# Attention, experts and feed-forward in one kernel: other places for operands, another order of weight splits, routing on GpSimd, stores by turns

## The chip, the cores and the metric

The kernel runs on one core of a Trainium2 chip. A core has TensorE (PE, with its weight load shown apart as PEld), VectorE (DVE), ScalarE (ACT), GpSimd (POOL) and SyncE (SP, which here only issues DMAs). The metric is the time on the device in microseconds (us), the median of the runs shown.

## What is computed

Three layers follow one another. Attention over 2 batches of 8 heads, 768 positions of 64 numbers, in which a query sees only the keys of its own cluster; a mixture of 8 experts in which each of 1536 tokens goes to one expert (512 to 1024 to 512); and a feed-forward layer (512 to 2048 to 512) whose activation is a quotient of two polynomials. All in fp32.

```python
mask = q_assign[:, :, :, None] == k_assign[:, :, None, :]     # argmax over 16 centroids
scores = np.where(mask, scale * np.matmul(q, k.transpose(0, 1, 3, 2)), -1000000000.0)
x = softmax(scores) @ v                                       # then (1536, 512)

expert_idx = np.argmax(xn @ en.T / tau, axis=1)
for e in range(E):
    mask = expert_idx == e
    out[mask] = gate_w[mask, None] * (np.maximum(x[mask] @ w1[e], 0.0) @ w2[e])

h = x @ w_in
P = a[0] + a[1] * h + a[2] * h**2 + a[3] * h**3
Q = 1.0 + np.abs(b[0]) * np.abs(h) + np.abs(b[1]) * h**2
return (P / (Q + 1e-06)) @ w_out
```

## The kernel before

**Split products.** A product in fp32 is made of three products of `fp32r` halves: an operand is split into a high part (a cast) and a low part (the operand less its high part), and PE multiplies high by high, high by low and low by high. Nearly all work of the other engines is such splitting. All instructions of one engine run in the order in which the program is written (`manual_schedule`), and each engine waits for the others by semaphores.

**Attention, 0 to about 287 us.** A unit is one head and one half of the queries (three blocks of 128); there are 32, and each takes six slots `t`, one for each block of 128 keys. In slot `t` PE transposes a block of probabilities (`transp`, L467); for the first block of a unit ScalarE copies it to `ptc` (L472, one buffer), GpSimd makes its high part `phi` and its low part `plo` (L72, L483); for the five others ScalarE casts `phi` (L475) and DVE subtracts (`plo`, L485). PE multiplies both with the values (L495, L496). At the end of a unit `pv_out` copies the sums of products and adds 1e-9 to the sum of exponentials (`ssum`: on GpSimd, L507, with a reciprocal on DVE six slots later, L512; on DVE, L504, with the reciprocal at once for the last two units, `FK`). `finish` divides, on DVE.

The task table `at(slot, fn)` puts everything else into the slots: heads' operands (`QBs`, `KBs`, `QAs`, `KAs`, three sets in turn, in the space of weight chunks 2 and 3 and three places beside them), the words of the feed-forward weights, routing, and the first expert's four weight chunks: `load_ahead` issues a chunk's load from SyncE into one of three `wraw` buffers, `early_hi` and `early_lo` split a quarter of it into the space of chunk 0 to 3 (L191 and L72 the casts, L197 the low parts). `early_split` does both.

**Routing** (`route`, a generator that is advanced now and then) takes three blocks of tokens at once: the largest logit, a one-hot row of it (L587, its fp32 copy L588), and its product with the token number (L590); then PE sums the one-hots, and GpSimd works out positions (L622, L623). The groups of batch 0 fall into the middle of attention, the last group of batch 1 behind its end.

**Experts, to about 476 us.** Expert 0 in part runs inside the end of attention (`eb_...`, L682). Experts 1 to 7 have four steps each: `expert_in`, `expert_relu` (high part on ScalarE, L1218, low part on DVE, L1220), `expert_out` of the step before. `weights(n)` splits the next `n` quarters of the ring of eight chunks (ScalarE L112, DVE L117), as far as their places are free. `row_gates` (the generators in `later`) works out the gate of an expert's rows: ScalarE reads the rows `xr` (L647), after which GpSimd may gather the next expert's rows into the same buffer (L666) and raises a sum to a power (L648).

**Feed-forward, to 752 us.** Three groups of four blocks of tokens, 16 steps each: `ff_in` (L1282), `poly_2` of the step before (ScalarE's logarithm and exponential L1430 and L1431, DVE L1432 to L1434), now and then a gather and transposes for the next group (`transpose_y`, L1265, with L1268 and L1270 on DVE), `poly_1` (ScalarE, DVE L1308 and L1310, GpSimd L1309), `poly_3` (splits the quotient: ScalarE L1442, GpSimd L1443 in the first group), `ff_out` three steps behind (L1455 to L1457), and `wide_part`, which splits quarters of the feed-forward weights from `yraw` (ScalarE L112, DVE L117). `ff_in` of a step takes one of two PSUM buffers, which L1310 of two steps before has read last. The loop's last line before is:

```python
            if i:
                wide_part(2 if i % 2 else 1)
```

At the end of a group the four results are copied and stored: by GpSimd's scatter in groups 0 and 1, from SyncE in the last group; the last block of all in two halves, one copied and stored by ScalarE, one copied by DVE and stored from SyncE.

## Time and profile before

| | |
|---|---|
| median of 3 runs | 761.67 us (760.78 to 762.51) |
| the profiled execution | 760.98 us, its span 759.3 us |
| PE busy | 734.6 us (97%) |
| DVE busy | 593.3 us (78%) |
| ACT busy | 565.0 us (74%) |
| POOL busy | 367.7 us (48%) |
| granted TensorE clock | 0.998 |

The span runs from the first to the last instruction of the profiled execution; 1.7 us of its time lie around it. A row of the timeline names start, length, engine, line, operation, what it writes and reads, and in brackets how long the engine had been idle and whose work ended that.

### The profile page before, as it was taken

How to read it: one execution, taken by the hardware profiler on the slowest of the kernel's cores; microseconds unless marked ns; L12 is line 12 of the kernel's file. 1: busy time of each engine (PE TensorE's matmuls, PEld its weight loads, DVE VectorE, ACT ScalarE, POOL GpSimd, SP SyncE). 2: the span in 40 equal slices, each digit the busy share in tenths (PEclk: the TensorE clock that was granted, in tenths of full speed). 3: DMA queues.
4: the chain of work that ended last, by engine and by line, in shares of the span. 5: the costliest groups of instructions: out<-in, count | busy, mean ns of one | idle time of the engine just before them, and what ended most of it. 6: DMA issues, size and time to landing. Idle time of an engine off the chain costs nothing.

```text
span 759.3 us, 12608 instructions
## 1 busy us (share of the span) xinstructions
PE 734.6 (97%) x4283; PEld 633.0 (83%) x4283; DVE 593.3 (78%) x1127; ACT 565.0 (74%) x1127; POOL 367.7 (48%) x462
## 2 busy tenths in 40 slices
PE   8999999999999999999999999999999999999996
PEld 5889999888889977889989999777888888888884
DVE  7778888898888877886676555589978788787774
ACT  5778888888888875885577555688877777777773
POOL 6798987888778872030221101266555332242220
PEclk9999999999999999999999999999999999999999
DMA  5677877867788265796775366222001110010001
GB/s 148 183 203 197 238 202 200 265 187 200 217 245 258 72 202 174 251 334 235 278 245 196 135 200 196 73 85 85 15 0 42 44 28 1 1 56 1 1 0 59
DMA packets 48712, 109.20 MB, mean 144 GB/s; under 512 B 6937, under 2 KB 10777, under 8 KB 48642
## 3 DMA queue, kind: packets, MB, share of 16 engines
q1 hardware_dynamic: 45618, 98.65, 42.4%
q0 software_dynamic: 2880, 9.55, 4.2%
q8 instruction: 35, 0.57, 0.3%
q14 instruction: 35, 0.29, 0.1%
q10 hardware_dynamic: 144, 0.13, 0.1%
HBM read 76.06 MB, written 18.99 MB: 125 GB/s over the span
## 4 chain that ended last, share of the span: by engine, by line
PE 71%; DVE 11%; ACT 6%; issue 4%; POOL 4%; DMA 3%; SPq 0%; POOLq 0%; ACTq 0%; DVEq 0%
PE pg L1282 14%; PE ph L1211 9%; PE pr L1457 5%; PE pr L1455 5%; PE pr L1456 5%; PE pt L467 4%; PE py L1242 3%; PE py L1241 3%; PE py L1240 3%; PE po_acc L495 2%; PE ps L449 2%; PE po_acc L496 2%; PE ps L450 2%; DVE plo L485 2%; DVE nm L452 2%
## 5 line engine op out<-in xcount | busy, mean ns | idle before, releaser
L1309 POOL TENSOR_TENSOR Bt<-Bt,A 128x512 f32<-128x512 f32 x46 | 59.7, 1297 | 147.4 <-ACT Bt L1307 147.4
L485 DVE TENSOR_TENSOR plo<-pt,phi 128x384 fp32r<-128x384 f32 x160 | 87.9, 550 | 20.9 <-ACT phi L475 18.4
L467 PE MATMUL pt<-ident,pr 128*128 128x128 f32 x576 | 96.3, 276 | 7.8 <-DVE plo L485 6.0
L475 ACT CAST phi<-pt 128x384 fp32r<-128x384 f32 x160 | 76.8, 482 | 32.2 <-PE pt L467 30.9
L1282 PE MATMUL pg<-x2hi,ck 128*128 128x512 f32 x368 | 92.7, 394 | 2.7 <-DVE Ct L1310 2.7
L452 DVE TENSOR_REDUCE nm<-ps 128x1 f32<-128x768 f32 x96 | 91.2, 950 | 5.3 <-PE ps L450 5.0
L458 ACT ACTIVATE pr<-ps,nm 128x768 f32<-128x768 f32 x96 | 87.4, 910 | 6.1 <-DVE nm L452 5.6
L467 PEld LDWEIGHTS pt<-ident,pr 128*128 128x128 f32 x576 | 70.7, 140 | 22.5 <-DVE plo L485 13.4
L1282 PEld LDWEIGHTS pg<-x2hi,ck 128*128 128x128 f32 x368 | 68.8, 188 | 19.4 <-DVE Ct L1310 4.0
L117 DVE TENSOR_TENSOR ck<-wraw,ck 128x512 fp32r<-128x512 f32 x112 | 71.1, 685 | 10.0 <-ACT ck L112 9.9
L1455 PE MATMUL pr<-ck,ghi 128*128 128x512 f32 x192 | 76.2, 397 | 0.0
L1457 PE MATMUL pr<-ck,glo 128*128 128x512 f32 x192 | 75.5, 393 | 0.0
L1456 PE MATMUL pr<-ck,ghi 128*128 128x512 f32 x192 | 75.4, 392 | 0.0
L495 PE MATMUL po_acc<-phi,vhl 128*128 128x384 f32 x192 | 72.9, 380 | 0.0
L496 PE MATMUL po_acc<-plo,vhl 128*128 128x384 f32 x192 | 65.0, 339 | 1.1 <-DVE plo L485 1.0
L112 ACT CAST ck<-wraw 128x512 fp32r<-128x512 f32 x112 | 62.5, 623 | 3.6 <-DMA wraw<-in_w_dram 3.3
L648 POOL TENSOR_TENSOR gss<-gss,half 128x2 f32<-128x2 f32 (+1 forms) x8 | 6.2, 777 | 119.8 <-ACT px L647 104.5
L1211 PE MATMUL ph<-xhi,ck 128*128 128x256 f32 x448 | 62.6, 282 | 0.0
L1432 DVE SCALAR_TENSOR_TENSOR Bt<-Bt,A 128x512 f32<-128x512 f32 (+1 forms) x48 | 32.7, 682 | 37.3 <-ACT A L1431 37.0
L1211 PEld LDWEIGHTS ph<-xhi,ck 128*128 128x128 f32 x448 | 59.0, 188 | 2.2
L1430 ACT ACTIVATE A<-Bt,qc 128x512 f32<-128x512 f32 (+1 forms) x48 | 34.3, 716 | 22.2 <-POOL Bt L1309 22.2
L1282 PE MATMUL pg<-x2lo,ck 128*128 128x512 f32 x184 | 49.9, 393 | 0.0
(331 smaller groups left out, 1937.6 us busy)
## 6 DMA issues: line engine op xcount, KB each, us to landing
wraw<-in_w_dram SPq DMA_DIRECT2D x32, 1024.0 KB, 6.4
words<-in_w_in_dram SPq DMA_DIRECT2D x16, 512.0 KB, 7.2
wf_d<-wz SPq DMA_DIRECT2D x32, 256.0 KB, 4.2
words<-in_w_out_dram SPq DMA_DIRECT2D x16, 512.0 KB, 7.4
yraw<-wf_d SPq DMA_DIRECT2D x16, 512.0 KB, 4.1
operands<-operands SPq DMA_DIRECT2D x40, 192.0 KB, 3.9
kq<-in_kqT_dram SPq DMA_DIRECT2D x16, 384.0 KB, 6.1
ys_d<-ysb SPq DMA_DIRECT2D x15, 260.0 KB, 4.3
```

What stands on the lines that cost most here:

```text
L452: dve.tensor_reduce(nm, ps[:, :, :HS], axis=AX.XY, op=ALU.max, negate=True)
L458: act.activation(pr.rearrange("p (a s) -> p a s", a=2), ps[:, :, :HS], AF.Exp, bias=nm[:, 0:1], accum_out=st["sum", u][:, qb:qb + 1])
L467: pe.transpose(t[:, j, :], st["P", u][j][:, kb * P:(kb + 1) * P], ident)
L475: act.copy(phi, tv)
L485: dve.tensor_tensor(plo, tv, phi.bitcast(F32), op=ALU.subtract)
L495: pe.matmul(o, w, phi, start=(kb == 1), stop=False)
L496: pe.matmul(o, w, plo, start=False, stop=(kb == 0))
L1211: pe.matmul(ph[:, f2, :], w[:, wx, k, c0:c0 + P], x[:, k, :], start=(i == 0), stop=(i == len(ops) - 1))
L1282: pe.matmul(ph, w[:, wx, k, c0:c0 + P], x[:, k, :], start=(i == 0), stop=(i == len(ops) - 1))
L1455: pe.matmul(o, ghi[:, s_], w[:, 0, k, :], start=(fb == 0), stop=False)
L1456: pe.matmul(o, ghi[:, s_], w[:, 1, k, :], start=False, stop=False)
L1457: pe.matmul(o, glo[:, s_], w[:, 0, k, :], start=False, stop=(fb == F2B - 1))
```

## The change

1. **Operands.** The three sets of a head's operands get other places in the space of chunks 2 and 3: set 0 now lies wholly in that of chunk 3, sets 1 and 2 in that of chunk 2, but for `QAs[2]`. The last head, 15, has set 0.
2. **End of attention.** Chunk 0 is split in slots 161 to 167 instead of 165 to 173; then chunk 2 in slots 171 to 177, ahead of chunk 1 in 175 to 180, with ScalarE and GpSimd taking the casts by turns and GpSimd all low parts; before, chunk 2 came last, and two of its low parts were on DVE. Chunk 3's casts stand in slots 183 to 187 instead of 191 to 193, and the three loads in slots 169, 184 and 187 instead of 174, 187 and 191.
3. **Sums.** For the last six units the 1e-9 is added on DVE, with the reciprocal at once; before, for the last two.
4. **Routing.** For batch 0's groups the one-hot, its copy and its product are made by GpSimd, in four operations instead of three on DVE. `dst_all` (L1270) goes from DVE to GpSimd too.
5. **First experts.** In the first four steps the ReLU stands ahead of the weights, in the first one `row_gates`' first part too; in expert 1 each `weights` call splits two quarters instead of three.
6. **Wide weights.** `wide_part` is not run in steps 1 and 2 and splits two quarters in steps 3 to 7, 9 and so on; before, two and one by turns from step 1.
7. **Last stores.** In the last group blocks go by turns from SyncE and ScalarE; the last block is copied whole by ScalarE and stored by it.

```diff
@@ -285,9 +285,9 @@
     scale = float(D) ** -0.5
     w2_, w3_ = (pools[j].tile([P, 8, 512], F32R, name=f"operands{j}", tag=f"ck{j}").rearrange("p a f -> p (a f)")
                 for j in (2, 3))
-    QBs = [w2_[:, j * S:(j + 1) * S] for j in range(3)]
-    KBs = [w2_[:, 3 * S:4 * S], w2_[:, 4 * S:5 * S], w3_[:, 0:S]]
-    QAs = [w3_[:, j * S:(j + 1) * S] for j in range(1, 4)]
+    QBs = [w3_[:, S:2 * S], w2_[:, 0:S], w2_[:, S:2 * S]]
+    KBs = [w3_[:, 2 * S:3 * S], w2_[:, 2 * S:3 * S], w2_[:, 3 * S:4 * S]]
+    QAs = [w3_[:, 3 * S:4 * S], w2_[:, 4 * S:5 * S], w3_[:, 0:S]]
     w0_ = pools[0].tile([P, 8, 512], F32, name="logits", tag="ck0")
     Ls = [w0_[:, j, 0:2 * NB * C].rearrange("p (g c) -> p g c", c=C) for j in range(2)]
     wz_ = [hp.tile([P, 512], I32, name=f"wz{j}", bufs=1) for j in range(6)]
@@ -500,7 +500,7 @@
         act.copy(ob, st["O", u])
         st["ob", u] = ob
         s = st["sum", u]
-        if u in FK:
+        if u >= n - 6:
             dve.tensor_scalar(s, s, 1e-9, None, op0=ALU.add)
             recip(u)
         else:
@@ -569,6 +569,7 @@
             return xpool.tile([P, 3, E], dt, name=name)
 
         last = k0 + 3 == NBT
+        eng = dve if b else pool
         rows = slice(g * 3, g * 3 + 3)
         dve.tensor_tensor(lt, lg2[:, rows, :, 0], lg2[:, rows, :, 1], op=ALU.add)
         store_x(b, g, slice((H - 1) * D, W))
@@ -584,10 +585,15 @@
         dve.tensor_reduce(m2, v, axis=AX.X, op=ALU.max)
         yield
         ohb = rE("rohb", BF16)
-        dve.tensor_tensor(ohb, v, m2.to_broadcast([P, 3, E]), op=ALU.is_equal)
-        dve.tensor_copy(oh, ohb)
+        if eng is dve:
+            dve.tensor_tensor(ohb, v, m2.to_broadcast([P, 3, E]), op=ALU.is_equal)
+            dve.tensor_copy(oh, ohb)
+        else:
+            pool.tensor_tensor(v, v, m2.to_broadcast([P, 3, E]), op=ALU.subtract)
+            pool.tensor_scalar(oh, v, 1.0, 0.0, op0=ALU.add, op1=ALU.max)
+            p_copy(ohb, oh)
         ot = rE("rot")
-        dve.tensor_tensor(ot, oh, tok1[:, k0:k0 + 3].unsqueeze(2).to_broadcast([P, 3, E]), op=ALU.mult)
+        eng.tensor_tensor(ot, oh, tok1[:, k0:k0 + 3].unsqueeze(2).to_broadcast([P, 3, E]), op=ALU.mult)
         yield
         yield True
 
@@ -986,15 +992,14 @@
         for j in range(3):
             at(131 + 12 * j, load_ahead, j)
         for j in range(4):
-            at((165, 167, 170, 173)[j], early_split, 0, j, pool, pool)
-            at((175, 177, 179, 181)[j], early_split, 1, j, pool, pool)
-            at((183, 185, 186, 187)[j], early_hi, 2, j, act)
-            at((184, 186, 187, 188)[j], early_lo, 2, j, dve if j > 1 else pool)
-        at(174, load_ahead, 3)
-        at(187, load_ahead, 4)
-        at(191, load_ahead, 5)
+            at((161, 163, 165, 167)[j], early_split, 0, j, pool, pool)
+            at((171, 172, 174, 177)[j], early_split, 2, j, (act, pool, pool, act)[j], pool)
+            at((175, 176, 179, 180)[j], early_split, 1, j, (pool, pool, act, pool)[j], pool)
+        at(169, load_ahead, 3)
+        at(184, load_ahead, 4)
+        at(187, load_ahead, 5)
         for j in range(3):
-            at(191 + j, early_hi, 3, j, act)
+            at((183, 185, 187)[j], early_hi, 3, j, act)
         at(144, first_rows_2)
         at(147, eb_gather)
         at(163, eb_x)
@@ -1267,7 +1272,7 @@
         act.copy(hi[:, :, c], t)
         dve.tensor_tensor(lo[:, :, c], t, hi[:, :, c].bitcast(F32), op=ALU.subtract)
         if k < SB:
-            dve.tensor_tensor(dst_all[:, k:k + 1], y[:, DM:DM + 1], never_all[:, k:k + 1], op=ALU.add)
+            pool.tensor_scalar(dst_all[:, k:k + 1], y[:, DM:DM + 1], never_all[:, k:k + 1], 1.0, op0=ALU.add, op1=ALU.mult)
 
     def ff_in(gi, fb):
         hi, lo = x2[gi]
@@ -1369,20 +1374,22 @@
             if p == FB // 2 - 1 and e + 1 < E:
                 transpose_x(e + 1)
             passed.add(("in", e, p))
+            if i < 4:
+                expert_relu(e, p)
             if i == 0:
-                expert_relu(e, p)
-            weights(3)
+                next(later[0])
+            weights(2 if e == 1 else 3)
             if e == E - 1:
                 expert_relu(e, p)
                 if p > 1:
                     for tb in range(2):
                         transpose_y(0, 2 * (p - 2) + tb, x2b)
-            if 0 < i and e < E - 1:
+            if 3 < i and e < E - 1:
                 expert_relu(e, p)
             if i:
                 expert_out(*steps[i - 1])
                 passed.add(("out", *steps[i - 1]))
-            weights(3)
+            weights(2 if e == 1 else 3)
             if e > 5:
                 wide_part(3, 4)
             if p == FB // 2 - 1 and e + 1 < E:
@@ -1460,22 +1467,14 @@
                 if tb % 2 == 0:
                     op["o"] = yraw[0].tile([P, 2, DM], F32, name="yraw", bufs=3)
                 y = op["o"][:, tb % 2]
-                if b == NBT - 1:
-                    half_ = slice(DM // 2, DM)
-                    act.activation(y[:, half_], o[:, half_], AF.Copy, scale=-1.0)
-                    act.dma_start(outs[NBT][b * P:(b + 1) * P, half_], y[:, half_])
-                    half_ = slice(0, DM // 2)
-                    dve.tensor_scalar(y[:, half_], o[:, half_], -1.0, None, op0=ALU.mult)
-                    sp.dma_start(outs[NBT][b * P:(b + 1) * P, half_], y[:, half_])
-                    continue
-                if tb % 2:
+                if tb % 2 and b < NBT - 1:
                     dve.tensor_scalar(y, o, -1.0, None, op0=ALU.mult)
                 else:
                     act.activation(y, o, AF.Copy, scale=-1.0)
                 if b < SB:
                     scatter(y, dst_all[:, b:b + 1], b)
                 else:
-                    sp.dma_start(outs[NBT][b * P:(b + 1) * P, :], y)
+                    (act if tb % 2 else sp).dma_start(outs[NBT][b * P:(b + 1) * P, :], y)
 
     left = nc.values_load(cnt_i[0:1, NBT:NBT + 1], min_val=0, max_val=NT)
     qc = const.tile([P, 1], F32, name="qc")
@@ -1498,8 +1497,8 @@
                 poly_3(*steps[i - 1])
             if i >= LAG:
                 ff_out(*steps[i - LAG])
-            if i:
-                wide_part(2 if i % 2 else 1)
+            if 3 <= i < 8 or i % 2:
+                wide_part(0 if i == 1 else 2)
         poly_2(*steps[-1])
         ff_out(*steps[-3])
         poly_3(*steps[-1])
```

PE's instructions stand in the same order before and after. Where the others change is shown at three places.

GpSimd, end of attention, before: `ck_4289` is chunk 1, `ck_4434` chunk 2; each pair of `phi` and `plo` is the first block of a unit.

```order
L72 TENSOR_SCALAR ck_4289<-wraw 128x512
L197 TENSOR_TENSOR ck_4289<-wraw,ck_4289 128x512
L507 TENSOR_SCALAR ssum<-ssum 128x3
L72 TENSOR_SCALAR ck_4289<-wraw 128x512
L197 TENSOR_TENSOR ck_4289<-wraw,ck_4289 128x512
L72 TENSOR_SCALAR ck_4289<-wraw 128x512
L197 TENSOR_TENSOR ck_4289<-wraw,ck_4289 128x512
L72 TENSOR_SCALAR phi<-ptc 128x384
L483 TENSOR_TENSOR plo<-ptc,phi 128x384
L72 TENSOR_SCALAR ck_4289<-wraw 128x512
L197 TENSOR_TENSOR ck_4289<-wraw,ck_4289 128x512
L507 TENSOR_SCALAR ssum<-ssum 128x3
```

And after (`ck_4219` is chunk 2, `ck_4298` chunk 1):

```order
L197 TENSOR_TENSOR ck_4219<-wraw,ck_4219 128x512
L72 TENSOR_SCALAR ck_4219<-wraw 128x512
L197 TENSOR_TENSOR ck_4219<-wraw,ck_4219 128x512
L72 TENSOR_SCALAR phi<-ptc 128x384
L483 TENSOR_TENSOR plo<-ptc,phi 128x384
L72 TENSOR_SCALAR ck_4219<-wraw 128x512
L197 TENSOR_TENSOR ck_4219<-wraw,ck_4219 128x512
L72 TENSOR_SCALAR ck_4298<-wraw 128x512
L197 TENSOR_TENSOR ck_4298<-wraw,ck_4298 128x512
L72 TENSOR_SCALAR ck_4298<-wraw 128x512
L197 TENSOR_TENSOR ck_4298<-wraw,ck_4298 128x512
L197 TENSOR_TENSOR ck_4219<-wraw,ck_4219 128x512
```

The sums L507 are gone from between the pieces, and chunk 2's pieces stand ahead of chunk 1's.

ScalarE, first two steps of expert 1, before (`ck_...` are weight chunks, L647 reads the rows):

```order
L1218 ACTIVATE hhi<-ph 128x512
L112 CAST ck_4988<-wraw 128x512 x4
L112 CAST ck_4999<-wraw 128x512 x2
L647 ACTIVATE px_5005,gss_5006<-xr 128x512 x2
L112 CAST ck_4999<-wraw 128x512 x2
L112 CAST ck_5045<-wraw 128x512
L1218 ACTIVATE hhi<-ph 128x512
L112 CAST ck_5045<-wraw 128x512 x3
L112 CAST ck_5101<-wraw 128x512 x3
L1218 ACTIVATE hhi<-ph 128x512
```

And after (L647 is now L653, L1218 is L1223):

```order
L1223 ACTIVATE hhi<-ph 128x512
L653 ACTIVATE px_4991,gss_4992<-xr 128x512 x2
L112 CAST ck_5000<-wraw 128x512 x4
L1223 ACTIVATE hhi<-ph 128x512
L112 CAST ck_5042<-wraw 128x512 x4
L662 ACTIVATE gv_4994,gmx_4993<-gv_4994,gss_4992 128x8 x2
L1223 ACTIVATE hhi<-ph 128x512
L112 CAST ck_5098<-wraw 128x512 x4
```

The two readers of `xr` stand ahead of the casts that they followed, and each ReLU has four casts behind it.

DVE, start of the feed-forward loop, from L1308 of step 1 on, before:

```order
L1308 TENSOR_TENSOR Ct<-Ct,px_6910 128x512
L1310 SCALAR_TENSOR_TENSOR Ct<-Ct,ab,px_6910 128x512
L117 TENSOR_TENSOR ck_6950<-yraw,ck_6950 128x512 x2
L1432 SCALAR_TENSOR_TENSOR Bt<-Bt,A 128x512
L1433 SCALAR_TENSOR_TENSOR A<-Bt,A 128x512
L1434 SCALAR_TENSOR_TENSOR Ct<-Ct,ab,A 128x512
L1308 TENSOR_TENSOR Ct<-Ct,pg 128x512
L1310 SCALAR_TENSOR_TENSOR Ct<-Ct,ab,pg 128x512
L117 TENSOR_TENSOR ck_6950<-yraw,ck_6950 128x512
L1432 SCALAR_TENSOR_TENSOR Bt<-Bt,A 128x512
L1433 SCALAR_TENSOR_TENSOR A<-Bt,A 128x512
L1434 SCALAR_TENSOR_TENSOR Ct<-Ct,ab,A 128x512
```

And after (L1308, L1310 and L1432 to L1434 are now L1313, L1315 and L1439 to L1441):

```order
L1313 TENSOR_TENSOR Ct<-Ct,px_6912 128x512
L1315 SCALAR_TENSOR_TENSOR Ct<-Ct,ab,px_6912 128x512
L1439 SCALAR_TENSOR_TENSOR Bt<-Bt,A 128x512
L1440 SCALAR_TENSOR_TENSOR A<-Bt,A 128x512
L1441 SCALAR_TENSOR_TENSOR Ct<-Ct,ab,A 128x512
L1313 TENSOR_TENSOR Ct<-Ct,pg 128x512
L1315 SCALAR_TENSOR_TENSOR Ct<-Ct,ab,pg 128x512
L1439 SCALAR_TENSOR_TENSOR Bt<-Bt,A 128x512
L1440 SCALAR_TENSOR_TENSOR A<-Bt,A 128x512
L1441 SCALAR_TENSOR_TENSOR Ct<-Ct,ab,A 128x512
L1313 TENSOR_TENSOR Ct<-Ct,pg 128x512
L1315 SCALAR_TENSOR_TENSOR Ct<-Ct,ab,pg 128x512
```

The low parts L117 of steps 1 and 2 are gone; they come later, in pairs.

## Rows read from the trace of the kernel before

**Rows 1.** Busy time by stretch: length, PE, PEld, DVE, ACT, POOL (instructions), clock, DMA share, GB/s.

```profile
255.00:291.00 36.00, 33.97 (x225) 29.82 (x223) 28.67 (x78) 27.81 (x64) 25.45 (x32) 1.00 0.46 148
...
535.00:751.00 216.00, 216.00 (x951) 176.06 (x950) 173.74 (x251) 160.53 (x251) 73.44 (x58) 1.00 0.05 17
```

**Rows 2.** Timeline, second routing group of batch 0: start, length, engine, line, [idle <-releaser].

```profile
194.41 1.84 POOL L330 TENSOR_TENSOR KA<-kq,operands 128x768 fp32r<-128x768 f32 x1
...
195.25 1.03 DVE L587 TENSOR_TENSOR rohb<-rv,rm 128x24 bf16<-128x24 f32 x1
...
197.50 0.44 PE L496 MATMUL po_acc<-plo,vhl 128*128 128x384 f32 x1 [0.95 <-DVE plo L485]
```

**Rows 3.** Timeline, end of attention.

```profile
247.70 0.52 POOL L72 TENSOR_SCALAR phi<-ptc 128x384 fp32r<-128x384 f32 x1 [2.33 <-ACT ptc L472]
...
272.73 1.01 POOL L483 TENSOR_TENSOR plo<-ptc,phi 128x384 fp32r<-128x384 f32 x1
...
276.00 0.18 DVE L512 RECIPROCAL rr<-ssum 128x3 f32<-128x3 f32 x1 [1.63 <-POOL ssum L507]
...
276.67 0.55 PE L467 MATMUL pt<-ident,pr 128*128 128x128 f32 x3 [0.86 <-DVE plo L485]
...
277.31 0.48 ACT L472 COPY ptc<-pt 128x384 f32<-128x384 f32 x1 [0.92 <-POOL ck L197]
...
279.96 1.25 DVE L504 TENSOR_SCALAR ssum<-ssum 128x3 f32<-128x3 f32 x1
...
281.92 0.55 PE L467 MATMUL pt<-ident,pr 128*128 128x128 f32 x3 [0.61 <-DVE plo L485]
```

**Rows 4.** GpSimd's groups, 246 to 282 us: line, count | busy, mean ns | idle before.

```profile
L197 POOL TENSOR_TENSOR ck<-wraw,ck 128x512 fp32r<-128x512 f32 x10 | 13.3, 1332 | 0.7
...
L72 POOL TENSOR_SCALAR ck<-wraw 128x512 fp32r<-128x512 f32 x8 | 5.0, 620 | 0.2
...
L507 POOL TENSOR_SCALAR ssum<-ssum 128x3 f32<-128x3 f32 x4 | 0.8, 197 | 0.3
```

**Rows 5.** Timeline, first steps of expert 1.

```profile
319.89 0.60 ACT L647 ACTIVATE px<-xr 128x512 f32<-128x512 f32 x1
...
321.28 1.65 ACT L112 CAST ck<-wraw 128x512 fp32r<-128x512 f32 x3
...
322.38 1.21 POOL L666 DMA_INDIRECT xr<-xd,row_tok  x1 [5.92 <-ACT ck L112]
...
324.46 0.50 PE L1242 MATMUL py<-ck,hlo 128*128 128x512 f32 x1 [0.19 <-DVE hlo L1220]
...
331.02 0.66 PE L672 MATMUL px<-ident,xr 128*128 128x128 f32 x4 [0.63 <-DMA xr<-xd,row_tok]
```

**Rows 6.** Timeline, feed-forward's first steps.

```profile
489.11 2.35 DVE L117 TENSOR_TENSOR ck<-yraw,ck 128x512 fp32r<-128x512 f32 x2
...
489.98 0.63 ACT L1431 ACTIVATE A<-A 128x512 f32<-128x512 f32 x1
...
495.01 1.19 PE L1282 MATMUL pg<-x2hi,ck 128*128 128x512 f32 x4 [1.62 <-DVE Ct L1310]
...
510.62 0.75 DVE L1310 SCALAR_TENSOR_TENSOR Ct<-Ct,ab,pg 128x512 f32<-128x512 f32 x1
...
516.49 0.75 DVE L1310 SCALAR_TENSOR_TENSOR Ct<-Ct,ab,pg 128x512 f32<-128x512 f32 x1
...
521.76 0.75 DVE L1310 SCALAR_TENSOR_TENSOR Ct<-Ct,ab,pg 128x512 f32<-128x512 f32 x1
...
527.79 1.00 DVE L1270 TENSOR_TENSOR dst_all<-y,never_all 128x1 int32<-128x1 f32 x1
...
530.23 0.97 PE L1282 MATMUL pg<-x2hi,ck 128*128 128x512 f32 x3 [1.08 <-DVE Ct L1310]
```

**Rows 7.** DMA issues, 735 to 760 us: count, KB each, median us to landing.

```profile
out_dram<-yraw SPq DMA_DIRECT2D x3, 256.0 KB, 3.3
...
out_dram<-yraw SPq DMA_DIRECT2D x1, 128.0 KB, 3.7
```

## The prediction

> **What bounds the kernel now.** I read the busy time by stage first [rows 1]: the reader is to compare the length of each stretch with PE's busy time in it. From 535 to 751 us PE is busy for all of 216.00 us (951 matmuls of mostly 512 columns, 0.227 us each), while 255 to 291 lacks 2.03 us of its 36. So PE sets the pace, its order of instructions is the same before and after, and the change can only be worth what it takes from PE's waits or adds to them. I then read its waits elsewhere one by one in the timeline and who ended each [rows 2, 3, 5, 6], and last how the stores land [rows 7].
>
> One effect runs through these rows. A small DVE operation on SBUF alone takes as long as the GpSimd operation beside it: the one-hot L587 took 1.03 us and ended 0.03 us after GpSimd's 1.84 us L330 [rows 2]; the sum L504, three numbers wide, took 1.25 us [rows 3]; L1270, one number wide, took 1.00 us [rows 6].
>
> **1. Batch 0's routing on GpSimd.** In the second group DVE's L587 lasts until 196.28; behind it come its two followers and only then the low part that PE waits 0.95 us for [rows 2]. All three leave DVE, so that low part can start when L452 ends, over 1 us earlier: the wait goes, -0.95. In the first group PE waits for none of the three: 0. On GpSimd four small operations, each about the 0.28 us of an L507 with its gap (0.8 us busy and 0.3 idle for four [rows 4]), some 1.1 us, stand ahead of the next high and low part; PE reads those one unit later, about 7 us, which hides them. Uncovered, they would cost those 1.1. Bounds -0.95 and +0.15; I take -0.95.
>
> **2. End of attention: splits, operands, sums.** The new places let chunk 2 be written after head 14 instead of head 15, so its splits move ahead of chunk 1's on GpSimd; two low pieces leave DVE; sums of units 26 to 29 go from GpSimd to DVE.
> Gains: DVE stood idle 1.63 us for GpSimd's late sum and PE then waited 0.86 [rows 3]; the 1.25 us sum, with chunk 2's pieces beside it, cost PE another 0.61 [rows 3]. Together -1.47.
> Against it: GpSimd works in order. Ahead of unit 30's low part (L483 at 272.73, ended 273.74 [rows 3]) stand 8 high and 11 low pieces instead of 7 and 7: 0.62 + 4 x 1.33 = +5.9 us [rows 4]. Three sums leave, 0.28 each: -0.8. I let GpSimd start one slot of the schedule earlier, 1.4 us, inside the 2.33 us that it idled before 247.70 [rows 3]. So it ends 3.7 us later, at 277.5. ScalarE's next copy into the same buffer (ptc, one buffer) began at 277.31 [rows 3] and must now wait for that: +0.2 on the old pace, so the 0.86 is not won, while the 0.61 is, since the two DVE pieces of that place are gone. Behind that copy on ScalarE are queued the casts that free PE's transposes. The moved sums may each be held by a GpSimd piece, 0.5 us of DVE on average (less than half of 1.33); PE is waiting for GpSimd by then, so I cost them at nothing; without that cover four of them cost up to 2. SyncE's load of chunk 3 is issued five slots earlier and waits for chunk 0's last piece; behind it stand word stores and row stores that nobody waits for soon: 0. Sum -0.61 + 0.2 = -0.4. Bounds: -1.5 if GpSimd keeps up, +3.7 if all its lateness shows.
>
> The Trainium skill (SBUF — State Buffer, section "SBUF: two separate sides") says that whichever of the two engines starts first holds the shared port pair for its whole instruction and the other blocks fully. By that rule every moved sum that meets a low piece may wait all of it, and this part would come to about +1 instead of -0.4. The rows of L587 and L504 bear the rule out; how often the four meet one, no row shows.
>
> **3. First experts.** GpSimd's gather of the next rows starts at 322.38, after 5.92 us of idle, when ScalarE has read the old rows (L647 from 319.89); PE then waits 0.63 us for the gathered rows [rows 5]. In the changed order L647 stands before six cast pieces, which at 1.65 us for three L112 [rows 5] puts the gather some 3.3 us earlier: the 0.63 goes. The ReLU ahead of the pieces takes away the 0.19 us wait for its low part [rows 5]. Four pieces a step instead of six still finish a chunk in every step of expert 1, one step ahead of its use. Sum -0.82, bounds -0.82 and +1.1; the matmuls of that step hide the two pieces that come later, and without them each such step would cost up to 1.1 us. The power operation behind the gathers moves with them, and holds DVE before the next ReLU's low part; worked out it ends 0.7 us ahead of need.
>
> **4. Wide weights later.** DVE's cycle is read from one L1310 to the next [rows 6]: a two-piece step takes 5.87 us (510.62 to 516.49), a one-piece step 5.27 (to 521.76). That L1310 ends at 522.51, and the next lets PE go at 530.23: 7.7 for the step with two pieces, transposes and L1270. PE's own step is 24 matmuls of 0.227 us [rows 1], about 5.5 with the first's fill. PE waited 1.62 at 495.01 and 1.08 at 530.23, each time for L1310 [rows 6].
> Without step 1's pair (2.35 us from 489.11, until 491.46) DVE goes on when ScalarE's exponential L1431 ends, 490.61: 0.85 earlier, so PE starts at 494.16 instead of 495.01 and the first wait is 0.77. Then comes one step without pieces (5.27: it is bound by the ScalarE and GpSimd chain): 499.4. Then five steps with pairs, where before twos and ones took turns: 505.3, 511.2, 517.0, 522.9 after four of them, and the fifth with the transposes, 7.7 less 0.9 for L1270, which goes to GpSimd: 529.7. PE by its own pace would be there at 494.16 + 6 x 5.5 + 0.6 for the transposes = 527.8, so it still waits for DVE: 529.7 instead of 530.2, -0.5 to -0.6. Later steps have slack (PE never waits behind 535 [rows 1]). What is late next is thus the same L1310. Bounds: +0.4 (each pair step 0.2 longer) and -2.7 (both waits gone); I take -0.55.
>
> **5. Last stores.** Both halves of the last block become one 256 KB store from ScalarE. The old last store, 128 KB, took 3.7 us to land, the three of 256 KB 3.3 [rows 7]: -0.4. ScalarE alone now copies the whole width, where DVE took a half: half of a 512-wide cast of 0.55 us (L112 [rows 5]), +0.27. Net -0.13. Bounds -0.4 and +0.4 (the landing no shorter, and the store that ScalarE now issues between its two copies in the way, which I put at 0.13 more).
>
> **The sum.** -0.95 - 0.4 - 0.82 - 0.55 - 0.13 = -2.85. The profiled execution took 760.98 (span 759.3 and 1.7 around it), 0.69 under the median of 761.67; on it the sum gives 758.1, on the median 758.8.
>
> **Rivals.**
> A, the sum as worked out: 757.8 to 759.8.
> B, GpSimd's lateness at the end of attention eats the gains of parts 1 and 2 (plo of unit 30 ends after 278.5 instead of 277.5): 761.67 - 0.82 - 0.55 - 0.13 + 0.2 = 760.4, up to 761.4. For it: GpSimd is busy 25.45 of 36 us there already [rows 1]. Against it: the idle time at 247.70.
> C, the pairs no longer hold DVE, because the chain of step 1 is shorter and the low parts on GpSimd fall elsewhere; both waits of the second feed-forward stage go: 758.8 - 2.15 = 756.7. For it: step 1 was the only pair right behind the stage's start. Against: the pair of 2.35 us and the long two-piece step later show the same hold [rows 6].
> D, slower: DVE's held sums and GpSimd's stretched low pieces hold each other. GpSimd's L197 has a mean of 1.33 us [rows 4]; if each of the 11 ahead of unit 30 is stretched by 0.45 (a third), its low part ends 5 us later, at 282.5, ScalarE's copy 5.2 us behind the old pace. It decides once GpSimd is more than some 2.5 us later than worked out: 761.67 - 2.5 + 5 = 764.2.
> E, the waits are replaced by others of the same size and nothing shows: 761.0 to 761.7.
>
> **How the numbers follow.** A 0.55, C 0.12, B 0.18, E 0.09, D 0.06. The time is A's, 758.8. For 8 in 10 the range reaches down into C, 757.0, and up to B's end, 761.4. A measurement of this kernel can tell about 0.2% from no change, which is 1.5 us, so faster means under 760.15: all of A and C, and little of B, 0.68; the rest of B and E are the same, 0.26; D is slower, 0.06.
>
> **What would show it.** Right: no L587 wait of PE in the second routing group; the gather of the first experts 3.3 us earlier without a PE wait; PE's first wait for L1310 about 0.8 us, then small ones, then about 0.9. At the end of attention PE's wait for the late sum replaced by ScalarE waiting for GpSimd before ptc. Wrong: a PE gap over 1.5 us between 265 and 285, feed-forward waits that vanish or grow beyond 2.7 us together, or a last store that lands over 4 us after its issue.

## The result: 754.16 us, over twice the gain that was forecast

| | before | after |
|---|---|---|
| median | 761.27 us (759.04 to 762.96, 6 runs) | 754.16 us (753.52 to 755.21, 6 runs) |
| profiled execution, span | 760.98, 759.3 us | 754.45, 752.7 us |
| PE, DVE, ACT, POOL busy | 734.6, 593.3, 565.0, 367.7 us | 733.4, 587.4, 562.9, 377.0 us |

The ratio is 0.991, with a 95% interval of 0.9895 to 0.9925: 6.9 us faster (0.009 x 761.27), 5.7 to 8.0. Forecast were 2.85 us and a range of 757.0 to 761.4; the time lies 2.8 us below it.

PE runs the same 4283 matmuls in the same order in both, so the start of each can be set against its start before. The difference is PE's lead; where it grows, time was won. The lead grew, by the steps of the prediction:

| place, in us of the trace before | lead gained | forecast |
|---|---|---|
| up to 195 us | 1.00 | 0 |
| second routing group, 197.5 | 1.23 | 0.95 |
| end of attention, 198 to 286 | 2.44 | 0.4 |
| first experts, 286 to 332 | 1.22 | 0.82 |
| feed-forward's start, 490 to 531 | 0.82 | 0.55 |
| from there to the last instruction | -0.09 | 0.13 |
| sum | 6.62, the spans' 759.3 - 752.7 | 2.85 |

Every sign of the first four steps was right, every size too small, and one of them by a factor of six. In busy time by stretch of the kernel after (length, then PE, PEld, DVE, ACT, POOL busy with their instructions, granted clock, DMA share, GB/s) the stretch of [rows 1] in which PE was busy for 33.97 us now has 35.44 of 36:

```profile
255.00:291.00 36.00, 35.44 (x234) 31.66 (x233) 29.80 (x89) 26.85 (x63) 26.08 (x32) 1.00 0.46 150
```

The timeline of the kernel after (start, length, engine, line, idle before and who ended it) at the places of [rows 2, 3, 5, 6]. First the second routing group:

```profile
193.42 1.84 POOL L330 TENSOR_TENSOR KA<-kq,operands 128x768 fp32r<-128x768 f32 x1
...
194.27 0.55 DVE L485 TENSOR_TENSOR plo<-pt,phi 128x384 fp32r<-128x384 f32 x1
...
195.22 0.23 POOL L592 TENSOR_TENSOR rv<-rv,rm 128x24 f32<-128x24 f32 x1
...
195.37 0.34 PE L496 MATMUL po_acc<-plo,vhl 128*128 128x384 f32 x1
```

GpSimd's 1.84 us L330 is the same, but no small DVE operation stands beside it; the low part is made at 194.27, PE's L496 starts without a wait and takes 0.34 us where it took 0.44 behind its wait of 0.95 [rows 2]. The end of attention:

```profile
269.73 0.69 DVE L504 TENSOR_SCALAR ssum<-ssum 128x3 f32<-128x3 f32 x1
...
271.13 0.55 PE L467 MATMUL pt<-ident,pr 128*128 128x128 f32 x3 [0.17 <-DVE plo L485]
...
273.44 1.01 POOL L483 TENSOR_TENSOR plo<-ptc,phi 128x384 fp32r<-128x384 f32 x1
...
273.69 0.49 PE L467 MATMUL pt<-ident,pr 128*128 128x128 f32 x3
...
274.48 0.48 ACT L472 COPY ptc<-pt 128x384 f32<-128x384 f32 x1
...
275.69 0.34 PE L496 MATMUL po_acc<-plo,vhl 128*128 128x384 f32 x1
...
276.12 0.32 DVE L504 TENSOR_SCALAR ssum<-ssum 128x3 f32<-128x3 f32 x1
...
276.48 0.17 DVE L512 RECIPROCAL rr<-ssum 128x3 f32<-128x3 f32 x1
...
277.96 0.49 PE L467 MATMUL pt<-ident,pr 128*128 128x128 f32 x3
```

DVE's sum and reciprocal stand together. PE's transposes at 273.69 and 277.96, those that waited 0.86 and 0.61 us before, have no wait. ScalarE's copy into `ptc` starts 0.03 us after GpSimd's low part has ended, so it follows GpSimd, as the prediction said, but PE doesn't wait for the copy. Something was also lost: the sum at 269.73 took 0.69 us beside GpSimd's pieces, where the last one takes 0.16, and PE's transposes at 271.13 waited 0.17 us for the DVE work behind it. The first experts and the feed-forward's start:

```profile
312.95 0.60 ACT L653 ACTIVATE px<-xr 128x512 f32<-128x512 f32 x1
...
314.19 1.10 POOL L672 DMA_INDIRECT xr<-xd,row_tok  x1 [2.32 <-ACT ck L112]
...
324.75 1.03 PE L678 MATMUL px<-ident,xr 128*128 128x128 f32 x8
...
488.33 2.11 PE L1287 MATMUL pg<-x2hi,ck 128*128 128x512 f32 x8 [0.83 <-DVE Ct L1315]
...
523.52 2.13 PE L1287 MATMUL pg<-x2hi,ck 128*128 128x512 f32 x8 [0.49 <-DVE Ct L1315]
```

The gather starts behind L653 at 314.19, and PE's transposes of the rows run as one group of eight, without the wait of 0.63 [rows 5]. The waits for L1310, now L1315, are 0.83 and 0.49 instead of 1.62 and 1.08 [rows 6]. The last stores (count, KB each, median us to landing):

```profile
out_dram<-yraw SPq DMA_DIRECT2D x2, 256.0 KB, 4.3
...
out_dram<-yraw ACTq DMA_DIRECT2D x2, 256.0 KB, 4.0
```

Both medians lie above the 3.7 and 3.3 of [rows 7]; in run 8, which has this part alone, they are 3.6 and 3.7.

### The profile page after: what moved, and what is told of

It reads as the page before. It is cut to its first block, busy times and chain, and to the rows that moved or that the text cites. A ratio compares the mean times of both kernels' runs of the same rounds, so it can differ in the third digit from the quotient of the medians.

```text
span 752.7 us, 12609 instructions
## 1 busy us (share of the span) xinstructions
PE 733.4 (97%) x4283; PEld 633.2 (84%) x4283; DVE 587.4 (78%) x1114; ACT 562.9 (75%) x1126; POOL 377.0 (50%) x477
## 4 chain that ended last, share of the span: by engine, by line
PE 77%; DVE 7%; POOL 5%; ACT 4%; issue 4%; DMA 2%; SPq 0%; ACTq 0%; POOLq 0%; DVEq 0%
PE pg L1287 14%; PE ph L1216 11%; PE pt L467 6%; PE pr L1462 5%; PE pr L1464 5%; PE pr L1463 5%; PE py L1247 3%; PE py L1245 3%; PE py L1246 3%; PE po_acc L495 3%; PE ps L449 3%; PE po_acc L496 3%; PE ps L450 3%; PE px L528 3%; PE pl L383 2%
## 5 line engine op out<-in xcount | busy, mean ns | idle before, releaser
L117 DVE TENSOR_TENSOR ck<-wraw,ck 128x512 fp32r<-128x512 f32 x112 | 70.9, 684 | 12.6 <-ACT ck L112 12.5
L450 PE MATMUL ps<-operands 128*128 128x384 f32 x192 | 64.9, 338 | 0.1
L496 PE MATMUL po_acc<-plo,vhl 128*128 128x384 f32 x192 | 64.7, 337 | 0.0
L1439 DVE SCALAR_TENSOR_TENSOR Bt<-Bt,A 128x512 f32<-128x512 f32 (+1 forms) x48 | 32.6, 679 | 39.8 <-ACT A L1438 39.8
```

The lines of the kernel that those rows point to most:

```text
L450: pe.matmul(o, d["QB"][:, q0:q0 + P], d["KB"][:, nh * HS:(nh + 1) * HS], start=False, stop=True)
L496: pe.matmul(o, w, plo, start=False, stop=(kb == 0))
```

## The experiments

Each part was run alone on the kernel before, or something was added to the kernel after. All times by the ratio to runs of before beside them.

| run | kernel | median, us | ratio, 95% | us against before |
|---|---|---|---|---|
| 1 | before + operands' places | 759.70 | 0.9995, 0.9980 to 1.0009 | -0.4 (-1.5 to +0.7) |
| 2 | before + places + splits | 763.70 | 1.0039, 1.0024 to 1.0054 | +3.0 (1.8 to 4.1) |
| 3 | before + sums | 760.06 | 0.9992, 0.9980 to 1.0004 | -0.6 (-1.5 to +0.3) |
| 4 | before + places + splits + sums | 757.92 | 0.9960, 0.9945 to 0.9976 | -3.0 (-4.2 to -1.8) |
| 5 | before + routing on GpSimd | 758.92 | 0.9981, 0.9970 to 0.9991 | -1.4 (-2.3 to -0.7) |
| 6 | before + first experts | 759.38 | 0.9981, 0.9971 to 0.9991 | -1.4 (-2.2 to -0.7) |
| 7 | before + wide weights | 759.66 | 0.9991, 0.9979 to 1.0003 | -0.7 (-1.6 to +0.2) |
| 8 | before + stores | 760.54 | 1.0001, 0.9989 to 1.0013 | +0.1 (-0.8 to +1.0) |
| 9 | after + two pieces on GpSimd | 756.51 | 0.9955, 0.9943 to 0.9967 | -3.4 (-4.3 to -2.5) |
| 10 | before + wide weights + `dst_all` | 759.69 | 0.9992, 0.9982 to 1.0002 | -0.6 (-1.4 to +0.2) |
| 11 | after, wide weights in single pieces | 759.61 | 0.9991, 0.9973 to 1.0008 | -0.7 (-2.1 to +0.6) |
| 12 | run 11, L330 in halves | 758.89 | 0.9982, 0.9971 to 0.9993 | -1.4 (-2.2 to -0.5) |
| 13 | after + one piece on GpSimd | 754.97 | 0.9926, 0.9909 to 0.9943 | -5.6 (-6.9 to -4.3) |
| 14 | after, single pieces, early enough | 753.17 | 0.9911, 0.9890 to 0.9932 | -6.8 (-8.4 to -5.2) |
| 15 | run 14, L330 in halves | 753.22 | 0.9901, 0.9885 to 0.9918 | -7.5 (-8.7 to -6.2) |

Runs 4, 5, 6, 10 and 8 are all parts of the change, each once: -3.0 - 1.4 - 1.4 - 0.6 + 0.1 = -6.3, within the interval of the whole. The end of attention is nearly half of it.

### Runs 1 to 4: the end of attention

The edit of run 3, which is also in run 4 and not in run 2:

```diff
-        if u in FK:
+        if u >= n - 6:
             dve.tensor_scalar(s, s, 1e-9, None, op0=ALU.add)
             recip(u)
```

Run 2 has parts 1 and 2 of the change (places, splits), run 1 the places alone.

> The kernel before with the operands' new places alone. In the two traces PE was already 1.0 us ahead at 195 us, before any moved split or routing step. Theory S (scatter: that 1.0 is the difference of two executions): the time is that of before within 0.5 us, and PE's start at a given instruction near 190 us lies within 0.5 us of before. Rival P (the places themselves shorten the first 200 us): 1.0 us faster, and PE is 1.0 us ahead near 190 us.

> Places and the new order of the four chunks' splits; the sums of units 26 to 29 stay on GpSimd. Theory G (GpSimd's line is the hinge, and the moved sums are what frees DVE from it): the sums L507 now stand behind more pieces, so DVE waits for them at two or more units, over 1.6 us each time, and the end of attention is 0.5 to 2 us slower than before. Rival Q (the pieces taken off DVE and the order make the gain, the sums hardly matter): 1.0 to 1.5 us faster than before.

> The sums of units 26 to 29 on DVE alone. Theory G: DVE's 1.63 us wait for the late sum and PE's 0.86 us wait go; 1.0 us faster, while the 0.61 us wait near 281.9 stays. Rival H (the moved sums are held by GpSimd's low parts, as the three-number sum of 1.25 us was): each takes 0.5 to 1.25 us of DVE, and the time is within 0.3 us of before.

> The whole change at the end of attention: places, splits and sums. Theory G: 2.0 to 2.5 us faster than before, with no wait of PE over 0.2 us between 265 and 285 us; more than the sum of the second and third experiment, since each part alone leaves a wait that the other takes away. Rival Q with scatter: 1.0 to 1.5 us faster, the rest of the 2.3 us of the changed kernel's trace being the difference of two executions.

Run 1's time is that of before, as theory S has it. Its trace leads by 1.4 us at 190 us, which S did not have. But the traces of runs 3, 7, 8 and 10, whose code is that of before up to there, lead by 0.4 to 1.0 as well, and run 6's trails by 0.6, so the profiled execution of before was behind most others in its first 160 us. By the time of run 1 and by these traces the 1.0 us that the changed kernel led at 195 is scatter of two executions, not a term.

Run 2 shows why the sums had to move. Its timeline, DVE's reciprocal and PE's transposes:

```profile
264.93 0.18 DVE L512 RECIPROCAL rr<-ssum 128x3 f32<-128x3 f32 x1 [2.56 <-POOL ssum L507]
...
273.98 0.17 DVE L512 RECIPROCAL rr<-ssum 128x3 f32<-128x3 f32 x1 [2.88 <-POOL ssum L507]
...
282.36 0.18 DVE L512 RECIPROCAL rr<-ssum 128x3 f32<-128x3 f32 x1 [2.17 <-POOL ssum L507]
...
265.60 0.55 PE L467 MATMUL pt<-ident,pr 128*128 128x128 f32 x3 [1.56 <-DVE plo L485]
...
274.66 0.55 PE L467 MATMUL pt<-ident,pr 128*128 128x128 f32 x3 [1.82 <-DVE plo L485]
...
283.03 0.55 PE L467 MATMUL pt<-ident,pr 128*128 128x128 f32 x3 [1.40 <-DVE plo L485]
```

Chunk 2's pieces put GpSimd so far behind that the sums L507 in its line reach DVE over 2 us late, three times, and PE with them: theory G, with a larger price than the 0.5 to 2 us expected. Run 3 takes away the first wait of [rows 3] (PE's start at 275.60 is 1.0 us better against its neighbours), but unit 30's sum, on DVE before as well, still stands beside DVE's own pieces, and in its trace a late gather took the gain back:

```profile
278.83 1.24 DVE L504 TENSOR_SCALAR ssum<-ssum 128x3 f32<-128x3 f32 x1
...
280.78 0.55 PE L467 MATMUL pt<-ident,pr 128*128 128x128 f32 x3 [0.74 <-DVE plo L485]
...
331.43 0.66 PE L672 MATMUL px<-ident,xr 128*128 128x128 f32 x4 [2.18 <-DMA xr<-xd,row_tok]
```

Run 4 has both parts, and 3.0 us, where the two alone have +3.0 and -0.6. In its trace PE wins 2.4 us between 255 and 286, after 0.35 lost behind a held sum. Each part is worth little or worse without the other: the splits need GpSimd's line free of sums, the sums need chunk 2's pieces off DVE. Rival Q falls by run 2. H is half right in run 3: of the four moved sums the last takes 0.98 us, the others 0.16 to 0.47, and the time lies between the two theories. In run 4 the longest takes 0.71, and no wait of PE over 0.2 us stands between 255 and 285.

### Runs 9 and 13: how much slack GpSimd had

```diff
+        for j in (0, 1):                  # run 13: j = 0 alone
+            at(177, early_lo, 2, j, pool)
         at(169, load_ahead, 3)
```

The added pieces compute low parts of chunk 2 a second time, in front of unit 30's.

> The changed kernel with two low parts of chunk 2 computed a second time on GpSimd, in front of unit 30's low part: 2.6 us more of GpSimd's time at the place that the prediction took for the hinge. Theory G (GpSimd's line has some slack there, about the 0.9 us by which ScalarE's copy precedes PE's next transposes into that buffer, and is then paid one for one): 1.2 to 2.0 us slower than the changed kernel, with one new wait of PE near 276 us and the copy into ptc 2.4 to 2.6 us later. Rival N (GpSimd is off the path there, the gain was DVE's alone): under 0.4 us slower.

> The changed kernel with one low part of chunk 2 computed a second time in front of unit 30's low part, 1.3 us of GpSimd. In the changed kernel that low part ends 1.24 us before PE reads it; with two more pieces PE waited 0.64 us for it and 0.3 us more behind it, and the granted clock then fell to 0.50 for 3.3 us. Theory K (a slack of 1.2 us, then one for one, and a clock drop only behind longer waits): one piece uses up the slack, PE waits 0.1 to 0.3 us, no clock drop, 0.0 to 0.5 us slower than the changed kernel. Rival N2 (no slack, half of every added piece shows): 1.0 to 1.5 us slower.

Run 9's timeline:

```profile
276.69 0.44 PE L495 MATMUL po_acc<-phi,vhl 128*128 128x384 f32 x1 [0.22 <-POOL phi L72]
...
276.72 1.00 POOL L483 TENSOR_TENSOR plo<-ptc,phi 128x384 fp32r<-128x384 f32 x1
...
277.75 0.48 ACT L472 COPY ptc<-pt 128x384 f32<-128x384 f32 x1 [2.61 <-POOL plo L483]
...
277.77 0.44 PE L496 MATMUL po_acc<-plo,vhl 128*128 128x384 f32 x1 [0.64 <-POOL plo L483]
```

And its busy time by stretch (the clock is the third number from the end):

```profile
276.00:279.00 3.00, 2.07 (x9) 1.00 (x7) 0.35 (x1) 1.25 (x3) 2.83 (x5) 1.00 1.02 297
...
279.00:283.00 4.00, 3.80 (x17) 3.61 (x17) 2.70 (x9) 1.51 (x5) 2.16 (x3) 0.57 0.83 271
```

PE waits for GpSimd's high and low part themselves, not for ScalarE's copy, though that waits 2.61 us: unit 30's product reads them before the copy's lateness reaches PE. Against the trace of the kernel after, PE falls back 2.0 us up to 279.3, and another 1.7 while the clock granted falls to 0.50 of full speed, the lower of its two levels (0.57 on average from 279 to 283). By the medians run 9 is 2.4 us slower than the kernel after, by the ratios 3.4.

Run 13's timeline:

```profile
275.47 0.49 PE L467 MATMUL pt<-ident,pr 128*128 128x128 f32 x3
...
276.47 1.01 POOL L483 TENSOR_TENSOR plo<-ptc,phi 128x384 fp32r<-128x384 f32 x1
...
277.51 0.48 ACT L472 COPY ptc<-pt 128x384 f32<-128x384 f32 x1 [1.38 <-POOL plo L483]
...
278.05 0.55 PE L467 MATMUL pt<-ident,pr 128*128 128x128 f32 x3
```

The transposes that waited 0.86 us before (275.47) have no wait. The copy waits 1.38 us, the next transposes but one start 0.06 us behind its end, PE falls back by 0.87 us in all at this place, and the clock stays at 1.00; the median is 0.8 us up (1.2 by the ratios, within their intervals). That lies between theory K and its rival: of 1.3 us added about 0.4 was slack, of the second 1.3 nearly all showed. So GpSimd was the hinge, as the prediction said, but with some 0.4 us to spare.

### Runs 5 and 6: routing and first experts

Run 5 has the routing part of the diff alone, run 6 that of the experts' loop.

> Batch 0's one-hot, its copy and its product on GpSimd, alone. Theory R (the wait goes whole, and what it costs PE is the start-to-start excess of 1.20 us, not the 0.95 us of idle time): 1.1 us faster, with all of the lead won at one place near 197 us; GpSimd's four operations cost PE nothing. Rival (GpSimd's next low part comes late): PE waits 0.5 us or more for it one unit later, and the time is 0.5 us faster or less.

> The first experts' order alone. Theory R: 1.2 to 1.4 us faster, the waits of 0.19 and 0.63 us gone with the excess around them (0.27 and 0.91 us in the comparison of the two traces). The prediction's reading (idle time alone): 0.8 us. Rival (the smaller weights calls come late): a PE wait between 335 and 400 us, and no gain.

Both as theory R has it. In run 5 the lead grows by 1.22 us at 197.5, and from there to 330 us only 0.1 of it is lost again: GpSimd's four operations are hidden.

In run 6 the lead grows by 0.47 and 0.85 us at the two waits, which is more than their idle time of 0.19 and 0.63 (the expectation had 0.27 and 0.91). And 0.63 was a lucky sample: in the nine traces with the old order (before, runs 1 to 5, 7, 8 and 10) that wait is 0.63 to 2.18 us, 1.04 on average.

### Runs 7, 10, 11 and 14: wide weights

Run 7 changes the loop's last lines as the diff does; run 10 also takes `dst_all` to GpSimd. Run 11 and run 14 have instead, on the kernel after:

```diff
-            if 3 <= i < 8 or i % 2:
-                wide_part(0 if i == 1 else 2)
+            wide_part({3: 1, 4: 1, 5: 2, 6: 1, 7: 2, 9: 2, 10: 1, 11: 2, 12: 1, 13: 2, 14: 1}.get(i, 0))   # run 11
+            if 2 <= i < 15:                                                                             # run 14
+                wide_part(2 if i in (5, 7, 9) else 1)
```

> The later splits of the feed-forward weights alone, with the sum for the scatter's targets (one number wide) still on DVE. Theory W (DVE's cycle sets the second wait): the first wait falls from 1.62 to 0.83 us; the five pair steps bring DVE to the transposes later than before, and with the held 1.00 us operation still in that step PE's second wait is about 1.5 us instead of 1.08: 0.1 to 0.5 us faster. Rival V (the pairs are hidden; that operation had no part in it): the second wait is 0.5 us, and the time 0.9 us faster.

> The later splits of the feed-forward weights and the scatter's targets on GpSimd, both, on the kernel before. The seventh experiment's trace has PE's second wait at 1.40 us with the held 1.00 us operation still on DVE. Theory W (that operation, held by a GpSimd product, is in DVE's cycle one for one): the second wait is 0.5 us, 0.8 to 1.0 us faster than before. Rival (GpSimd's operation now holds DVE in its turn): the second wait stays above 1.0 us.

> The changed kernel with the same 16 quarters split in other steps: one in steps 3, 4, 6, 10, 12 and 14, two in 5, 7, 9, 11 and 13. Theory W (a pair step takes DVE 5.87 us, a single one 5.27, PE's own step is 5.5): no pair debt is left at the transposes, PE's second wait of 0.49 us goes, and with its restart 0.6 to 0.9 us faster than the changed kernel; the first wait of 0.83 us stays. Rival (the second wait is the transposes' own): 0.2 us or less.

> The changed kernel with 16 quarters split one in each of steps 2 to 14, two in 5, 7 and 9, so that the twelfth, the last that step 12 multiplies by, is done in step 10 instead of in step 11 as in the eleventh kernel, where PE waited 3.36 us for its cast and then ran at half clock. Theory W (a pair of pieces is a debt of 0.4 us of DVE, a single one is none): the second wait of 0.49 us and the small ones before it go as in the eleventh, no wait at step 12; 0.6 to 1.3 us faster than the changed kernel. Rival (DVE's debt comes due at the transposes instead): a wait of 0.4 us or more between 523 and 545 us and 0.3 us or less.

PE's waits in the feed-forward's first 60 us, of run 7, of run 10 and of run 14, where the first wait is the only one:

```profile
495.68 2.11 PE L1282 MATMUL pg<-x2hi,ck 128*128 128x512 f32 x8 [0.83 <-DVE Ct L1310]
...
531.78 2.13 PE L1282 MATMUL pg<-x2hi,ck 128*128 128x512 f32 x8 [1.40 <-DVE Ct L1310]
```

```profile
494.94 2.12 PE L1282 MATMUL pg<-x2hi,ck 128*128 128x512 f32 x8 [0.84 <-DVE Ct L1310]
...
530.15 2.12 PE L1282 MATMUL pg<-x2hi,ck 128*128 128x512 f32 x8 [0.49 <-DVE Ct L1310]
```

```profile
487.36 2.11 PE L1287 MATMUL pg<-x2hi,ck 128*128 128x512 f32 x8 [0.84 <-DVE Ct L1315]
```

Run 7 against run 10: the one-number operation on DVE, held by GpSimd's product, was worth 0.91 us of PE's second wait. Their times, -0.7 and -0.6, do not show it, so it rests on one trace of each. Run 14: with single pieces that wait is gone, so it was the debt of the pairs, and not of the transposes (theory W). PE leads the trace after by 1.4 us more at 524 than at 490. Run 11 had the same gain and lost it again: I counted the twelfth piece in time when it is split in step 11, but step 12 starts with the matmuls that read it, and its cast stands behind step 11's other work on ScalarE. Run 11's timeline, and its busy time in the stretch behind:

```profile
536.62 1.13 ACT L112 CAST ck<-yraw 128x512 fp32r<-128x512 f32 x2
...
537.29 3.29 PE L1287 MATMUL pg<-x2hi,ck 128*128 128x512 f32 x6 [3.36 <-ACT ck L112]
```

```profile
537.00:541.00 4.00, 3.71 (x9) 2.49 (x10) 3.96 (x5) 2.01 (x4) 3.38 (x3) 0.57 0.03 6
```

PE waits 3.36 us, and then runs at a granted clock of 0.50 again, for (1 - 0.57) x 4 / 0.5 = 3.4 us.

### Runs 8, 12 and 15: stores, and GpSimd's long operation in halves

Run 8 has the stores' part of the diff. Runs 12 and 15 (on runs 11 and 14) split the operation beside which routing's small operations were held (the edit is shortened):

```diff
-        (dve if first else pool).tensor_tensor(lo, kq, hi.bitcast(F32), op=ALU.subtract)
+        for c in (slice(0, S // 2), slice(S // 2, S)):        # the first head stays on DVE
+            pool.tensor_tensor(lo[:, c], kq[:, c], hi[:, c].bitcast(F32), op=ALU.subtract)
```

> The last group's stores alone. By the two traces PE ended 6.7 us earlier and the last instruction 6.6 us earlier, so the stores gain nothing before the last instruction: within 0.3 us of before. Rival: the landing of the last store counts behind the last instruction and is 0.4 us shorter, 0.3 to 0.5 us faster.

> The eleventh kernel, and GpSimd's subtraction of 128x768 for a head's operands (1.84 to 2.0 us, which holds small DVE operations beside it until it ends) made in two halves. Theory L (DVE is let in between two GpSimd operations): the waits of 1.01 us near 158 us and of 0.63 us near 209 us shrink to half or less; 0.5 to 1.2 us faster than the eleventh, if GpSimd's 14 further operations cost nothing. Rival (DVE loses to the second half too): 0 to 0.5 us slower.

> The fourteenth kernel with GpSimd's 128x768 subtraction in two halves. In the twelfth the routing operation that was held for 1.10 us took 0.28 us, and PE's wait behind it fell from 1.01 to 0.19 us. Theory L (it is the length of one GpSimd operation that holds DVE): 0.6 to 1.0 us faster than the fourteenth. Rival (the further GpSimd operations take as much back elsewhere): within 0.3 us of the fourteenth.

The stores are worth nothing that can be measured. As for the halves, DVE is indeed let in between them. First the kernel after, where L582 waits out GpSimd's whole operation, then run 15 (L586 is the same operation, L334 the two halves):

```profile
157.29 1.84 POOL L330 TENSOR_TENSOR KA<-kq,operands 128x768 fp32r<-128x768 f32 x1
...
158.07 1.10 DVE L582 SCALAR_TENSOR_TENSOR rv<-rv,iote 128x24 f32<-128x24 f32 x1
...
159.90 0.55 PE L467 MATMUL pt<-ident,pr 128*128 128x128 f32 x3 [1.01 <-DVE plo L485]
```

```profile
157.72 1.98 POOL L334 TENSOR_TENSOR KA<-kq,operands 128x384 fp32r<-128x384 f32 x2
...
158.49 0.27 DVE L586 SCALAR_TENSOR_TENSOR rv<-rv,iote 128x24 f32<-128x24 f32 x1
...
159.50 0.55 PE L471 MATMUL pt<-ident,pr 128*128 128x128 f32 x3 [0.18 <-DVE plo L489]
```

The operation takes 0.27 us instead of 1.10, and PE's wait behind it 0.18 instead of 1.01. The expectation's other wait, 0.63 us near 209, stays at 0.63 in runs 12 and 15: there DVE's L625, 1.07 us long in both, starts beside the cast L72 ahead of the subtraction, which was not cut. Run 12's median is 0.7 us below run 11's, and their intervals overlap. And run 15 is no faster than run 14: its trace wins 0.8 us at 159 and loses more in small steps at 35 to 43, 142, 172 and 260 to 272 us. Whether the further GpSimd operations cause these is open; the rival's time is what came.

Runs 14 and 15 have medians 1.0 us below the kernel after (753.17 and 753.22 against 754.16), and all five runs of 15 (752.66 to 753.50) lie below all six of the kernel after; but beside them the kernel before ran 0.95 us faster too (760.32 against 761.27), and the intervals of their ratios overlap its own. They are the best of the case, and not shown to be faster.

## Why the prediction was wrong

**What bounds the kernel**: right. PE's waits were the whole of it, and the gain is what came off them. **Part 1, routing**: right in place and cause; 0.95 was too small by the traces, which both have 1.2; run 5's time has 1.4, with an interval (0.7 to 2.3) that holds 0.95 too.

**Part 2, end of attention**: the step that failed, -0.4 against 3.0 measured (run 4; 2.4 in the trace after), beyond even its bound of 1.5. The order of things was right: GpSimd works in order, the copy into `ptc` waits for unit 30's low part, the moved sums free DVE. Wrong were how late GpSimd is, and what that lateness costs PE. First the lateness. GpSimd's busy time (the fifth) up to the end of that low part, before from 236 us, and after from 234, where PE is at the same matmul:

```profile
236.00:273.74 37.74, 37.15 (x257) 34.20 (x256) 32.98 (x65) 32.99 (x76) 32.73 (x48) 1.00 0.50 164
```

```profile
234.00:274.45 40.45, 39.67 (x274) 36.44 (x272) 37.14 (x76) 36.80 (x84) 37.51 (x50) 1.00 0.46 155
```

And its low parts of weights in these two stretches (count | busy, mean ns):

```profile
L197 POOL TENSOR_TENSOR ck<-wraw,ck 128x512 fp32r<-128x512 f32 x7 | 9.0, 1290 | 0.6
```

```profile
L197 POOL TENSOR_TENSOR ck<-wraw,ck 128x512 fp32r<-128x512 f32 x11 | 14.1, 1289 | 0.7
```

The work grew by 37.51 - 32.73 = 4.8 us, where I had 5.9 - 0.8 = 5.1: the 1.33 us that I took for a piece was a mean over a later piece stretched to 1.74; the others take 1.29. GpSimd's idle time fell from 5.01 to 2.94 us, by 2.1, where I let only 1.4 be filled, from the one wait that I had a row for. So the low part came 2.7 us later and not 3.7: at 274.45, which is 276.4 on before's clock (PE's lead there is 2.0), instead of 277.5.

Then its cost. I had ScalarE's copy due at 277.31 and took the wait of 0.86 us as not won once the low part ends at 277.5. Run 13 is that case: its low part ends at 277.48, which is 277.7 on before's clock, and still the 0.86 is won, and PE falls back 0.87 us behind it. So at the lateness of the prediction this part would have brought some 1.5 us in the trace, not 0.4: the microsecond of lateness is worth at most 0.9 of the 2.0 us that were missed. The rest are waits that I priced too low or left out. The two large ones gave 1.08 and 0.82 us of lead, small ones 1.2 (0.5 of it at 284.85 and 285.74, which had 0.08 and 0.12 us of idle time), and 0.6 was lost behind two held sums.

The sentences on the Trainium skill (SBUF — State Buffer, section "SBUF: two separate sides") made the term +1. Of the four moved sums in the trace after, two were held, for 0.60 and 0.69 us, and PE's transposes behind them started 0.29 and 0.33 us late. I had put the holds at nothing, because PE would be waiting for GpSimd by then; it was not, and they cost 0.6, less than half of the 1.4 that lies between -0.4 and +1. The trace agrees with the rule on the holding (L582 above takes 1.10 us beside one operation, and 0.27 where that is cut); how much of a hold reaches PE it does not say.

**Part 3, first experts**: right that the gather comes some 3.3 us earlier (322.38 to 314.19 less PE's lead of 4.7 is 3.5). The term was 0.82; run 6 has 1.4 (0.7 to 2.2), the two traces 1.2 to 1.3.

**Part 4, wide weights**: the term of 0.55 agrees with run 10 (0.6, -0.2 to 1.4) and is near the trace (0.8), in part by luck. Its working was half right: the first wait is 0.83 for the 0.77 worked out, but the second is 0.49, where I had PE 1.9 us early; part of the debt was paid in small waits on the way. **Part 5, stores**: -0.13 against nothing measurable; the step that had the last store land in 3.3 instead of 3.7 us is wrong, they took 4.0 and 4.3 (3.6 and 3.7 in run 8).

**A second error runs through all terms**: I took a wait's price from the idle time in brackets. The lead shows more: for the five waits that went whole, 0.95, 0.86, 0.61, 0.19 and 0.63 of idle, 3.24 in all, PE's lead grew by 1.23, 1.08, 0.82, 0.47 and 0.85, 4.45 in all. The matmul behind a wait also takes longer itself (0.44 for 0.34 in the routing rows, 0.55 for 0.49 for the transposes). Read from the starts of PE's instructions, the terms 0.95, 0.61 and 0.82 of the sum would have been 1.0 us larger together. The range missed for the same reasons: its low end was C, a rival on the feed-forward, and no case had the end of attention gain its 1.5 us bound.

Of the rivals, B and D (GpSimd's lateness eats the gain) fell by runs 4 and 13, though run 9, whose low part ends at 278.9 on before's clock, beyond B's 278.5, shows B's mechanism: the gain of part 2 is gone there, 1.7 us of it by the clock; C did not come in its own form; E fell with the result.

## What to carry to other kernels

Price a wait by PE's start against the pace of its neighbours, not by the idle time in brackets, and take it from more than one execution where a DMA is in it: one wait here was 0.63 to 2.18 us by the execution. When work is moved onto an engine that runs in order, sum that engine's idle time over the whole stretch in which the moved work may start, before saying how late the next thing is. Two edits that each cost or bring nothing can be worth 3 us together, when one makes the line late and the other takes its customers out of it.

## What the runs showed of the hardware that was not expected

- A short wait of PE can cost a second time. In run 9, after 1.1 us of PE's waits within three microseconds, the longest of 0.64, the granted clock fell from 1.00 to 0.50 (2.4 to 1.2 GHz) for about 3.4 us and cost 1.7 us more; in run 11 the same followed a wait of 3.36 us. In run 7's trace the same drop (199.6 to 203.0 us) began 2 us behind a wait of 0.97 at 197.1 and cost 1.2; before and runs 1, 3, 6, 8 and 10 have that wait too, 0.95 to 0.99, and no drop. In run 2 waits of 1.40 to 1.82 us were followed by none, nor in run 13 waits of 0.3. What decides is not settled here.
- GpSimd lets a held DVE operation in between two of its own that stand back to back: 1.10 us became 0.27 when a 1.84 us operation was cut in two.
